# Attention scores with two heads side by side in the rows of TensorE's array

## The chip, the cores and the metric

One core of one Trainium2 chip runs the whole kernel in one launch. The metric is the time on the device in microseconds (us); the times below are those of single executions of the same kernel. One further execution was profiled; the rows come from it.

## The reference, cut to what matters

Three layers are computed one after the other for 1536 tokens: attention with a local window, a gated layer, and a mixture of 8 experts of which each token takes two. The change is in the attention:

```
B, H, S, D = q.shape                      # 2, 8, 768, 64
scores = matmul(q, k.T) / sqrt(D)
keep   = (column < n_global) | ((row - column >= 0) & (row - column < n_local))   # 8, 96
scores = where(keep, scores - slope[h] * dist, -1e9)
a      = exp(scores - max);  a /= sum(a) + 1e-9
x      = matmul(a, v)                     # then: rms norm, gate/value/out, experts
```

## The kernel before, in words

A tile `ti` is 128 tokens (12 tiles: 2 batches of 6). Because of the window, a tile looks at 256 columns of keys (`W`): 32 columns that hold the first keys of the batch, the end of the tile before, and its own 128. The first tile of each batch looks at 128. Tiles 0 to 5 (`F32T` is 6) work in fp32, where a product of the program is two matmul records in the profile; tiles 6 to 11 split each operand into a high and a low part in fp32r and add three products (`prods`), one record each.

A slot is two heads of one tile, so there are 4 slots to a tile and 48 in all, `u = 4 * ti + pr`. For a tile, `prep` turns k and q so that the head dimension lies on partitions: two heads of 64 share the 128 partitions of one block (4 blocks for 8 heads). For a slot, `scores` multiplies, VectorE adds the bias and takes the maximum (L436), ScalarE takes exp (L439); `turn` (fp32) or a DMA (`dma_start_transpose`, L448, on SP's queue) turns the result, and `values` multiplies with v. At a tile's end come rms norm (its power on POOL, L585) and `norm`, which turns x for the next layer.

How the two heads reach the array. In tile 0 (`ti < HALF`), a head's 64 partitions of q and of k are multiplied as they lie, so a matmul uses half of the array's rows; `pair` puts heads h and h + 2 in a slot, and both have the same half. In tiles 1 to 11, q is held in two copies (`qtile`), one for even and one for odd heads, in which the other head's 64 partitions are zero; the matmul then uses all 128 rows, and the zeros keep the other head out. The copies' zeros are written once by POOL (L345, L347), and `prep` fills each copy's other half by an operation of its own: high part on ScalarE or VectorE (L387, L389), low part on VectorE (L395).

PSUM has 8 banks, named by tag: `g`, `v`, `s`, `t`, `t2`, `o` and two of `d`. The first 12 slots (`START`, the call's `wide`) run before the next layer begins, in an order written out in `early` (every TensorE instruction follows the one before it, `seq`). There the scores of a slot (both heads in one bank) alternate between `g` and `s`, and q is turned in a `d` bank. From slot 12 on, the work of the attention is mixed with that of the next layer (`VISITS`, lines 698 to 745, which holds `g`, `v` and both `d`), in an order that a planner makes from its own estimate of times; scores then have the bank `s` alone, and all transposes share `t` and `t2`. Each engine works off its instructions in the order of the program. `busy` adds matmuls on zeros in the first slots. The tag `pt`, two buffers, holds the turned exp values between `turn` or the DMA and `values`, which comes up to three slots later (L540).

Of the kernel before, what the change touches and what calls it, by code (L numbers as in the profile page):

```python
# [10 lines left out]
F32 = mybir.dt.float32  # L11
F32R = mybir.dt.float32r
F16 = mybir.dt.float16
# [8 lines left out]
P = 128  # L22
# [85 lines left out]
def fused(ctx: ExitStack, tc: tile.TileContext, q, k, v, n_global, n_local, w_gate, w_val, w_out,  # L108
# [8 lines left out]

    def pair(ti, pr):

        a, b = (pr // 2, pr % 2) if ti < HALF else (pr % 2, pr // 2)  # L120
        return (4 * a + b, 4 * a + b + 2)
    DC = DM // P
# [12 lines left out]
    START = 12  # L135
    HALF = 1
    WARM = 4
# [26 lines left out]
    def build_bias():  # L164
        rel = sb.tile([P, 2 * P], F32, name="rel", tag="n2", bufs=N2)
        msk = sb.tile([P, 2 * P], F32, name="msk", tag="s", bufs=4)
        work = at.tile([P, 2, 2 * P], F32, name="work", tag="p", bufs=2)
        tmp, rel0, msk0 = work[:, 0], work[:, 1, :P], work[:, 1, P:]
        nc.gpsimd.iota(rel, pattern=[[-1, 2 * P]], base=P, channel_multiplier=1,
                       allow_small_or_imprecise_dtypes=True)  # L170
        nc.vector.tensor_scalar(msk, rel, 0.0, None, op0=ALU.is_ge)
        nc.vector.tensor_scalar(tmp, rel, float(n_local), None, op0=ALU.is_lt)
        nc.vector.tensor_mul(msk, msk, tmp)
        nc.vector.tensor_scalar(rel0, rel[:, P:], -float(n_local), None, op0=ALU.add)
        nc.vector.tensor_mul(rel0, rel0, msk[:, P:])
        nc.vector.tensor_scalar(rel0, rel0, float(n_local), None, op0=ALU.add)
        nc.vector.tensor_copy(msk0, msk[:, P:])
        if n_global > 0:
            nc.vector.memset(msk0[:, :n_global], 1.0)
            nc.vector.memset(rel[:, :n_global], float(n_local))  # L180
            nc.vector.memset(msk[:, :n_global], 1.0)
        if n_global < 32:
            nc.vector.memset(msk[:, n_global:32], 0.0)
        nc.vector.tensor_scalar(msk, msk, -BIG, BIG, op0=ALU.mult, op1=ALU.add)
        nc.vector.tensor_scalar(msk0, msk0, -BIG, BIG, op0=ALU.mult, op1=ALU.add)
        nc.vector.tensor_add(rel0, rel0, msk0)
        for h in (0, 2, 1, 3, 4, 6, 5, 7):
            nc.vector.tensor_scalar(nbias0[:, h, :], rel0, slopes[h], None, op0=ALU.mult)
        nc.vector.tensor_add(rel, rel, msk)
        return rel  # L190
# [49 lines left out]
    def busy(k):  # L240

        if k and state.get("strict"):
            pz = ps.tile([P, 512], F32, name="idle", tag="v")
            for _ in range(k):
                seq(nc.tensor.matmul(pz.rearrange("p (a b) -> p a b", a=4), blank,
                                     blank.rearrange("p (o d) -> p o d", o=1).broadcast_to([P, 4, P]), start=True, stop=True))
# [51 lines left out]

    cyc = {"s": 0, "t": 0, "o": 0, "d": 0}

    def bank(kind, wide, name):
        tags = {"s": ("g", "s"), "t": ("t", "t2"), "o": ("o", "d"), "d": ("d",)} if wide else {"s": ("s",), "t": ("t", "t2"), "o": ("o",)}
        cyc[kind] += 1
        tag = tags[kind][cyc[kind] % len(tags[kind])]
        return ps.tile([P, 512], F32, name=name, tag=tag, bufs=2 if tag == "d" else 1)

# [28 lines left out]

    def qtile(x, m, ti):

        key = x, m, ti // NB
        if key not in qz:
            one = m == "e"  # L340
            full = ti < F32T
            qz[key] = t = at.tile([P, NP, P], F32 if full else F32R, name=f"q{x}{m}{ti}", tag=f"q{x}{m[0]}", bufs=1 if one else 2)
            r = slice(D, P) if one else slice(0, D)
            if full:
                zero = nc.gpsimd.memset(t[r], 0.0)  # L345
            else:
                zero = nc.gpsimd.tensor_scalar(t[r], ident[r].rearrange("p (o d) -> p o d", o=1).broadcast_to([D, NP, P]),  # L347
                                               0.0, None, op0=ALU.mult)
            follow(zero.ins, state["pool"])
        return qz[key]  # L350

    def prep(ti, wide, hook=None):
# [9 lines left out]
        else:  # L362
            kT = [at.tile([P, NP, 2 * P], F32R, name=f"kT{ti}_{x}", tag=f"kT{x}", bufs=2) for x in range(2)]
        if ti < HALF:
            qa = at.tile([P, NP, P], F32, name=f"qT{ti}", tag="q1o", bufs=2)
            qT = {(0, h): qa[(h % 2) * D:(h % 2 + 1) * D, h // 2, :] for h in range(H)}
            qd = [(slice(0, P), qa, None)]
        else:
            qb = [[qtile(x, m, ti) for m in ("e", f"o{ti % 2}")] for x in range(1 if full else 2)]
            qT = {(x, h): qb[x][h % 2][:, h // 2, :] for x in range(len(qb)) for h in range(H)}  # L370
            qd = [(slice(m * D, (m + 1) * D), qb[0][m], qb[-1][m]) for m in range(2)]
        operands = ((kn, [(slice(0, P), kT[0][:, :, P:], kT[1][:, :, P:])], 1.0), (qn, qd, -(D ** -0.5)))
        p3s = {}
        state["cur", ti] = (W, C0, nblk, kT, qT)
        for step, (cs, src, dst, sc) in enumerate([(slice(0, NP),) + o for o in operands] if ti else
# [4 lines left out]
            if sc not in p3s:  # L380
                p3s[sc] = bank("t" if sc == 1.0 or not wide else "d", wide, f"pt{ti}").rearrange("p (a b) -> p a b", a=NP)
            p3 = p3s[sc]
            for c in range(cs.start, cs.stop):
                seq(nc.tensor.transpose(p3[:, c, :], src.rearrange("p (a t) d -> p a (t d)", a=NP)[:, c, :], ident))  # L384
            for n, (rs, dh, dl) in enumerate(dst):
                if wide and n:
                    nc.vector.tensor_scalar(dh[rs, cs], p3[rs, cs], sc, None, op0=ALU.mult)  # L387
                else:
                    nc.scalar.activation(dh[rs, cs], p3[rs, cs], AF.Copy, scale=sc)  # L389
                if full:  # L390
                    continue
                if sc == 1.0:
                    nc.vector.tensor_sub(dl, p3, dh.bitcast(F32))
                else:
                    nc.vector.scalar_tensor_tensor(dl[rs], p3[rs], sc, dh[rs].bitcast(F32), op0=ALU.mult, op1=ALU.subtract)  # L395

# [15 lines left out]
    def scores(u, wide):  # L412
# [6 lines left out]
        nb = nbias if ti % NB else nbias0  # L419
        psc = bank("s", wide, f"ps{ti}_{pr}")  # L420
        first = ti < F32T
        if first:
            pp = at.tile([P, 2, 2 * P], F32, name=f"p{ti}_{pr}", tag="p", bufs=2)
        else:
            pp = at.tile([P, 2, 2, W], F16, name=f"h{ti}_{pr}", tag="p", bufs=2)
        for t in range(2):
            h = pair(ti, pr)[t]
            sl = slice((h % 2) * D, (h % 2 + 1) * D) if ti < HALF else slice(0, P)
            o = psc[:, t * W:(t + 1) * W]
            prods = ((0, 0), (1, 0), (0, 1)) if ti >= F32T else ((0, 0),)  # L430
            for n, (a, c) in enumerate(prods):
                seq(nc.tensor.matmul(o, qT[a, h], kT[c][sl, h // 2, C0:], start=(n == 0), stop=(n == len(prods) - 1)))  # L432
        for t in range(2):
            h = pair(ti, pr)[t]
            s = sb.tile([P, 2 * P], F32, name=f"s{ti}_{h}", tag="s", bufs=4)
            state["s"] = nc.vector.tensor_tensor_reduce(s[:, :W], nb[:, h, :], psc[:, t * W:(t + 1) * W], 1.0, BIG * 10,  # L436
                                                        op0=ALU.add, op1=ALU.min, accum_out=mx[:, h:h + 1]).ins
# [6 lines left out]
        if first:  # L444
            state["p", u] = pp
            return
        both = at.tile([P, 2, 2, nblk, P], F16, name=f"ph{ti}_{pr}", tag="pt", bufs=2)
        nc.sync.dma_start_transpose(both.rearrange("p x t j q -> p (x t j) q"), pp.rearrange("p x t c -> p (x t c)"))  # L448
        state["pt", u] = both[:, 0], both[:, 1]

    def turn(u, wide):
        ti, pr = divmod(u, NP)
        nblk = state["cur", ti][2]
        pp = state.pop(("p", u))
        ptt = bank("t", wide, f"pp{ti}_{pr}")
        p4 = ptt.rearrange("p (t j q) -> p t j q", t=2, j=2)
        for t in range(2):
            for j in range(nblk):
                seq(nc.tensor.transpose(p4[:, t, j, :], pp[:, t, j * P:(j + 1) * P], ident))
        pf = at.tile([P, 2, 2, P], F32, name=f"pf{ti}_{pr}", tag="pt", bufs=2)  # L460
        if pr % 2 == 0:
# [9 lines left out]
    def values(u, wide):  # L471
# [15 lines left out]
        if pr == 0:  # L487
            state["po", ti] = bank("o", wide, f"po{ti}")
        po = state["po", ti]
        for t in range(2):  # L490
            h = pair(ti, pr)[t]
            hs = slice(h * D, (h + 1) * D)
# [52 lines left out]
    def early(n):  # L545
# [19 lines left out]
        if n < NP:  # L565
            for h in pair(0, n):
                follow(nc.vector.tensor_scalar(nbias[:, h, :], rel, slopes[h], None, op0=ALU.mult).ins, state["s"])
# [27 lines left out]
    def norm(ti, x, wide):  # L595
        pt = bank("t", wide, f"px{ti}")
        p3 = pt.rearrange("p (a b) -> p a b", a=DC)
# [564 lines left out]
    n = 0  # L1162
# [224 lines left out]
```

## Time and profile before

| | |
|---|---|
| time, median of 3 runs | 762.61 us (761.08 to 763.19) |
| the profiled execution's own time | 762.32 us |
| its span, first to last instruction | 760.5 us |
| TensorE busy (matmul) | 735.9 us, 97% of the span |
| weight loads | 666.6 us, 88% |
| VectorE, ScalarE, POOL busy | 485.8, 410.2, 318.8 us |

Attention ends about 195 us into the span; the rest is the two expert layers. A busy TensorE is counted from modelled ends of matmuls that overlap, so the distance between the starts of two records tells more than their durations.

### The profile page before, as it was taken

The numbers are of one execution on the slowest core, as the hardware profiler recorded it, in microseconds if no ns is written. First come the engines' busy times: TensorE is split into PE (matmuls) and PEld (weight loads), VectorE is DVE, ScalarE is ACT, GpSimd is POOL, SyncE is SP. The second block draws the span as 40 slices with busy tenths as digits, with TensorE's granted clock in tenths as the row PEclk, the third lists the DMA queues.
The fourth block names the chain that finished last, engine by engine and source line by source line (L and its number), as shares of the span: only waits on it lengthen the run. The fifth ranks groups of instructions, "written<-read, shape, count | busy, mean of one in ns | idle before, by whom it ended". The sixth has DMA issues, their size and how long they took to land.

```text
span 760.5 us, 13550 instructions
## 1 busy us (share of the span) xinstructions
PE 735.9 (97%) x4763; PEld 666.6 (88%) x4763; DVE 485.8 (64%) x1134; ACT 410.2 (54%) x878; POOL 318.8 (42%) x350
## 2 busy tenths in 40 slices
PE   9999989999999999999999999999999999999993
PEld 6788989889988888889999989888999999999993
DVE  5998899885497888334535568844555646665641
ACT  5777778675454443114332456536676757776630
POOL 3348853421476566001543144562234345353411
PEclk9999999999999999999999999999999999999997
DMA  8454457533243840002234511989396979898611
GB/s 199 126 166 126 119 135 152 97 85 70 89 135 111 250 137 1 1 6 106 56 57 91 188 29 49 310 240 281 88 264 186 281 175 285 206 323 169 212 41 37
DMA packets 183159, 107.98 MB, mean 142 GB/s; under 512 B 114193, under 2 KB 165393, under 8 KB 183088
## 3 DMA queue, kind: packets, MB, share of 16 engines
q1 hardware_dynamic: 174240, 84.61, 43.0%
q0 software_dynamic: 7120, 19.32, 7.8%
q10 hardware_dynamic: 1728, 3.15, 1.3%
q8 instruction: 39, 0.64, 0.4%
q14 instruction: 32, 0.26, 0.1%
HBM read 75.23 MB, written 16.49 MB: 121 GB/s over the span
## 4 chain that ended last, share of the span: by engine, by line
PE 79%; DVE 7%; DMA 5%; issue 4%; ACT 2%; POOL 1%; SPq 0%; POOLq 0%; ACTq 0%; DVEq 0%
PE pz L1041 17%; PE pz L705 14%; PE acc L732 12%; PE ac L1081 11%; PE pg L705 5%; PE pv L705 5%; PE ac L1058 5%; PE ps L432 3%; PE po L500 1%; DMA ph<-h 1%; PE lg L816 1%; DMA rv<-in_moe_w_val_dram 1%; PE pt L384 1%; PE po L496 1%; DMA y<-out_dram,ic 1%
## 5 line engine op out<-in xcount | busy, mean ns | idle before, releaser
L1041 PE MATMUL pz<-gh,sa 128*128 128x256 f32 (+7 forms) x576 | 154.0, 335 | 2.0 <-POOL sa L686 1.3
L1041 PEld LDWEIGHTS pz<-gh,sa 128*128 128x128 f32 x576 | 103.6, 188 | 7.3 <-POOL sa L686 1.8
L1041 PE MATMUL pz<-gl,sa 128*128 128x256 f32 (+7 forms) x288 | 96.4, 335 | 0.0
L732 PE MATMUL acc<-wo,dh 128*128 128x512 f32 x288 | 88.8, 399 | 0.7 <-ACT dh L718 0.5
L1081 PE MATMUL ac<-zh,sb 128*128 128x480 f32 (+4 forms) x320 | 84.7, 357 | 0.0
L1048 ACT ACTIVATE zh<-pz 128x256 fp32r<-128x256 f32 (+7 forms) x72 | 35.2, 488 | 80.5 <-PE pz L1041 80.5
L1049 DVE SCALAR_TENSOR_TENSOR zl<-pz,zh 128x256 fp32r<-128x256 f32 (+7 forms) x72 | 39.7, 552 | 58.3 <-ACT zh L1048 58.0
L705 PE MATMUL pz<-xTh,wg 128*128 128x256 f32 x352 | 73.9, 286 | 1.3 <-ACT wg L653 1.3
L705 PE MATMUL pz<-xTh,wv 128*128 128x256 f32 x352 | 73.6, 287 | 0.0
L1114 POOL DMA_INDIRECT out_dram<-y,me x30 | 34.2, 1141 | 72.6 <-DVE y L1110 68.7
L1081 PEld LDWEIGHTS ac<-zh,sb 128*128 128x128 f32 x320 | 59.6, 188 | 3.2
L705 PEld LDWEIGHTS pz<-xTh,wg 128*128 128x128 f32 x352 | 58.3, 190 | 3.8 <-ACT wg L653 1.5
L719 POOL TENSOR_TENSOR dl<-u,dh 128x256 fp32r<-128x256 f32 (+1 forms) x38 | 36.9, 972 | 56.6 <-ACT dh L718 31.9
L686 DVE TENSOR_TENSOR sb<-wab,sb 128x512 fp32r<-128x512 f32 x67 | 47.4, 707 | 19.7 <-ACT sb L682 16.8
L686 DVE TENSOR_TENSOR sa<-wab,sa 128x512 fp32r<-128x512 f32 x60 | 44.6, 745 | 23.6 <-ACT sa L682 23.1
L682 ACT ACTIVATE sa<-wab 128x512 fp32r<-128x512 f32 x72 | 44.9, 625 | 27.4 <-PE ac L1081 14.0
L732 PEld LDWEIGHTS acc<-wo,dh 128*128 128x128 f32 x288 | 51.2, 189 | 9.3 <-ACT dh L718 0.7
L705 PEld LDWEIGHTS pz<-xTh,wv 128*128 128x128 f32 x352 | 57.9, 190 | 0.3
L1041 PEld LDWEIGHTS pz<-gl,sa 128*128 128x128 f32 x288 | 54.1, 188 | 2.6 <-DVE gl L1013 0.3
L732 PE MATMUL acc<-wo,dl 128*128 128x512 f32 x144 | 53.5, 397 | 0.0
L1081 PE MATMUL ac<-zl,sb 128*128 128x480 f32 (+4 forms) x160 | 52.4, 358 | 0.0
L1058 PE MATMUL ac<-sb,zh 128*128 128x512 f32 (+1 forms) x176 | 50.6, 375 | 0.0
(255 smaller groups left out, 1841.8 us busy)
## 6 DMA issues: line engine op xcount, KB each, us to landing
wab<-in_moe_w_dram SPq DMA_DIRECT2D x128, 256.0 KB, 6.3
rg<-in_moe_w_gate_dram SPq DMA_DIRECT2D x12, 512.0 KB, 4.5
rv<-in_moe_w_val_dram SPq DMA_DIRECT2D x12, 512.0 KB, 3.6
ro<-in_moe_w_out_dram SPq DMA_DIRECT2D x12, 512.0 KB, 3.6
vn<-in_v_dram SPq DMA_DIRECT2D x12, 256.0 KB, 3.8
out_dram<-zero SPq DMA_DIRECT2D x1, 3072.0 KB, 14.0
x2d<-x ACTq DMA_DIRECT2D x12, 256.0 KB, 5.0
x2p<-hw SPq DMA_DIRECT2D x12, 256.0 KB, 4.6
```

Of the source, the lines that this page charges most:

```text
L432: seq(nc.tensor.matmul(o, qT[a, h], kT[c][sl, h // 2, C0:], start=(n == 0), stop=(n == len(prods) - 1)))
L682: cp = nc.scalar.activation(wp[:, 0], src, AF.Copy)
L686: sub = (nc.gpsimd if pool else nc.vector).tensor_sub(wp[:, 1], src, wp[:, 0].bitcast(F32))
L705: mm = nc.tensor.matmul(pz, a[:, cs], x[:, tt:tt + nt, c, :], start=(n == 0), stop=(n == 3 * DC - 1))
L719: (nc.gpsimd if ci < len(CHUNKS) - 1 else nc.vector).tensor_sub(dl, u, dh.bitcast(F32))
L732: nc.tensor.matmul(acc[t], a[:, tt], w, start=(f == CHUNKS[ci][0] and n == 0), stop=(end and n == 2))
L1041: mm = nc.tensor.matmul(pz[:, :cap], a[:, cs], x[:, c, :cap], start=(k == 0), stop=(k == 3 * DC - 1))
L1048: self.act = nc.scalar.activation(dh[:, :cap], pz[:, :cap], AF.Relu).ins
L1049: nc.vector.scalar_tensor_tensor(dl[:, :cap], pz[:, :cap], 0.0, dh[:, :cap].bitcast(F32), op0=ALU.max, op1=ALU.subtract)
L1058: mm = nc.tensor.matmul(o, a[:, s * P:s * P + m], w[:, cuts(s)[x]], start=(f == 0 and k == 0), stop=(f == FB2 - 1 and k == 2)).ins
L1081: nc.tensor.matmul(acc[c][:, :cap], w[:, c * P:(c + 1) * P], a[:, :cap], start=(f == 0 and k == 0), stop=(f == FB2 - 1 and k == 2))
L1114: st = nc.gpsimd.indirect_dma_start(out=out, out_offset=bass.IndirectOffsetOnAxis(ap=self.me[:m, s, 0:1], axis=0), in_=y[:m], in_offset=No ...
```

## The change

All tiles use the half of the array in which a head's partitions lie. The zero-padded copies of q (`qtile`), `pair` and `HALF` are gone; a slot holds heads 2 * pr and 2 * pr + 1, which lie in the two different halves, and their products are issued in turn, one for each head. The two heads write to two different banks: pairs (`g`, `s`) and (`v`, one `d`) alternate in the first 12 slots, and (`s`, `t2`) is the only pair afterwards, so that transposes have `t` alone from there on. The other `d` bank of the first slots (`spare`) serves `busy` and every second output of `values`; q is turned in `t` or `t2`. From slot 12 on, the first product of a slot waits for the VectorE operation that read the last scores and for the low part of q, and the other products follow in order. `prep` has one operation for the high part of q and one for the low part, over all 128 partitions. The tag `pt` has three buffers.

```diff
-    def qtile(x, m, ti):
...
+    def score_banks(u, wide):
+        if ("ps", wide) not in state:
+            tags = (("g", "s"), ("v", "d")) if wide else (("s", "t2"),)
+            state["ps", wide] = [[ps.tile([P, 512], F32, name=f"ps{u}{x}", tag=x, bufs=2 if x == "d" else 1) for x in xs] for xs in tags]
+        banks = state["ps", wide]
+        return banks[u % len(banks)]
...
+    def bank(kind, name):
+        tags = ("t", "t2") if ("ps", False) not in state else ("t",)
+        cyc[kind] += 1
+        if kind == "o":
+            return spare() if state.get("strict") and cyc[kind] % 2 == 0 else ps.tile([P, 512], F32, name=name, tag="o")
+        return ps.tile([P, 512], F32, name=name, tag=tags[cyc[kind] % len(tags)])
...
-        if ti < HALF:
-            qa = at.tile([P, NP, P], F32, name=f"qT{ti}", tag="q1o", bufs=2)
...
-            qb = [[qtile(x, m, ti) for m in ("e", f"o{ti % 2}")] for x in range(1 if full else 2)]
+        qa = [at.tile([P, NP, P], F32 if full else F32R, name=f"qT{ti}_{x}", tag=f"q{x}", bufs=2) for x in range(1 if full else 2)]
+        qT = {(x, h): qa[x][(h % 2) * D:(h % 2 + 1) * D, h // 2, :] for x in range(len(qa)) for h in range(H)}
...
-            for n, (rs, dh, dl) in enumerate(dst):
-                if wide and n:
-                    nc.vector.tensor_scalar(dh[rs, cs], p3[rs, cs], sc, None, op0=ALU.mult)
...
+            dh, dl = dst
+            nc.scalar.activation(dh[:, cs], p3[:, cs], AF.Copy, scale=sc)
+            if not full:
+                state["prepped", ti] = nc.vector.scalar_tensor_tensor(dl[:, cs], p3[:, cs], sc, dh[:, cs].bitcast(F32), op0=ALU.mult,
+                                                                      op1=ALU.subtract).ins
...
+        out_s = [b[:, :W] for b in score_banks(u, wide)]
...
+        for n, (a, c) in enumerate(prods):
+            for t in range(2):
+                mm = seq(nc.tensor.matmul(out_s[t], qT[a, 2 * pr + t], kT[c][t * D:(t + 1) * D, pr, C0:], start=(n == 0),
+                                          stop=(n == len(prods) - 1))).ins
+                if not state.get("strict"):
+                    if n or t:
+                        follow(mm, state["mm"])
+                    else:
+                        for x in (state["s"], state.get(("prepped", ti))):
+                            if x is not None:
+                                hold(mm, x)
+                    state["mm"] = mm
-            for n, (a, c) in enumerate(prods):
-                seq(nc.tensor.matmul(o, qT[a, h], kT[c][sl, h // 2, C0:], start=(n == 0), stop=(n == len(prods) - 1)))
...
-        both = at.tile([P, 2, 2, nblk, P], F16, name=f"ph{ti}_{pr}", tag="pt", bufs=2)
+        both = at.tile([P, 2, 2, nblk, P], F16, name=f"ph{ti}_{pr}", tag="pt", bufs=3)
...
-        pf = at.tile([P, 2, 2, P], F32, name=f"pf{ti}_{pr}", tag="pt", bufs=2)
+        pf = at.tile([P, 2, 2, P], F32, name=f"pf{ti}_{pr}", tag="pt", bufs=3)
```

## Rows read from the trace of the kernel before

**Rows 1.** The page: busy us per engine, and the last chain's shares by engine.
```profile
PE 735.9 (97%) x4763; PEld 666.6 (88%) x4763; DVE 485.8 (64%) x1134; ACT 410.2 (54%) x878; POOL 318.8 (42%) x350
...
PE 79%; DVE 7%; DMA 5%; issue 4%; ACT 2%; POOL 1%; SPq 0%; POOLq 0%; ACTq 0%; DVEq 0%
```

**Rows 2.** Busy us by stretch: PE, PEld, DVE, ACT, POOL, granted clock, DMA share, GB/s.
```profile
36.00:95.00 59.00, 56.30 (x421) 52.26 (x421) 50.38 (x135) 44.25 (x120) 41.82 (x43) 1.00 0.51 141
...
104.00:190.00 86.00, 83.25 (x906) 77.87 (x906) 68.17 (x203) 59.16 (x180) 28.21 (x39) 1.00 0.49 102
190.00:760.00 570.00, 555.21 (x3183) 504.31 (x3181) 331.68 (x668) 277.54 (x492) 232.55 (x222) 0.99 0.52 147
```

**Rows 3.** Waits of PE, first 190 us: us in total, times, longest.
```profile
PE po L500 <- DMA ph<-h: 1.5, 2, 0.9
PE ps L432 <- DVE mx L436: 1.3, 2, 1.1
PE pz L705 <- ACT wg L653: 1.3, 1, 1.3
...
PE px L599 <- DVE x L586: 1.1, 1, 1.1
PE pp L459 <- DVE pf L464: 1.0, 1, 1.0
PE pp L459 <- DVE xTl L605: 0.7, 1, 0.7
PE po L496 <- ACT pf L462: 0.5, 1, 0.5
```

**Rows 4.** The chain that ended last, first 190 us: start us, us, what.
```profile
39.39 0.70 DVE q0o L387
...
60.74 0.86 PE ps L432 x4
...
107.97 2.29 DMA ph<-h
...
127.70 0.71 PE ps L432 x6
...
166.44 4.22 DMA ph<-h
```

**Rows 5.** Timeline at the score matmuls of tile 0's last slot and of tile 1.
```profile
14.33 0.28 PE L496 MATMUL po<-vn,pf 128*128 128x64 f32 x1
14.54 0.18 PEld L432 LDWEIGHTS ps<-kT,qT 64*128 64x128 f32 x1
...
14.75 0.49 PE L432 MATMUL ps<-kT,qT 64*128 64x128 f32 x3
...
14.97 0.27 PE L432 MATMUL ps<-kT,qT 64*128 64x128 f32 x1
15.17 0.10 PEld L245 LDWEIGHTS <-zero 128*128 128x128 bf16 x1
15.18 0.39 PE L245 MATMUL idle<-zero 128*128 128x512 bf16 x1
...
18.08 0.28 PE L496 MATMUL po<-vn,pf 128*128 128x64 f32 x1
...
18.19 0.43 PE L432 MATMUL ps<-kT,q0e 128*128 128x256 f32 x1
```

**Rows 6.** Lines that fill or clear q: duration ns min/median/max, first and last start.
```profile
L387 DVE TENSOR_SCALAR q0o<-pt x3: 694/695/695, 14.9 to 39.4; 64x512 f32<-64x512 f32 x3
...
L389 ACT ACTIVATE q0o<-pt x8: 592/593/596, 50.9 to 159.1; 64x512 fp32r<-64x512 f32 x6, 64x512 f32<-64x512 f32 x2
...
L395 DVE SCALAR_TENSOR_TENSOR q1o<-pt,q0o x6: 694/694/696, 84.9 to 160.9; 64x512 fp32r<-64x512 f32 x6
...
L347 POOL TENSOR_SCALAR q0o<-ident x2: 1934/1936/1937, 70.4 to 87.4; 64x512 fp32r<-64x512 f32 x2
```

**Rows 7.** Waits of SP's own queue, whole span: us in total, times, longest.
```profile
SPq L448 <- PE po L500: 6.5, 6, 2.1
```

More of the change, by code (lines that the diff above doesn't have):

```diff
@@ L116, in fused @@
     NP = H // 2
-    def pair(ti, pr):
-        a, b = (pr // 2, pr % 2) if ti < HALF else (pr % 2, pr // 2)
-        return (4 * a + b, 4 * a + b + 2)
     DC = DM // P
@@ L186, in build_bias @@
         nc.vector.tensor_add(rel0, rel0, msk0)
-        for h in (0, 2, 1, 3, 4, 6, 5, 7):
+        for h in range(H):
             nc.vector.tensor_scalar(nbias0[:, h, :], rel0, slopes[h], None, op0=ALU.mult)
@@ L242, in busy @@
         if k and state.get("strict"):
-            pz = ps.tile([P, 512], F32, name="idle", tag="v")
+            pz = spare()
             for _ in range(k):
@@ L297, in halves, with spare @@
         return w[:, :, 0], w[:, :, 1]
-    cyc = {"s": 0, "t": 0, "o": 0, "d": 0}
-    def bank(kind, wide, name):
-        tags = {"s": ("g", "s"), "t": ("t", "t2"), "o": ("o", "d"), "d": ("d",)} if wide else {"s": ("s",), "t": ("t", "t2"), "o": ("o",)}
+    cyc = {"t": 0, "o": 0}
+    def bank(kind, name):
+        tags = ("t", "t2") if ("ps", False) not in state else ("t",)
         cyc[kind] += 1
-        tag = tags[kind][cyc[kind] % len(tags[kind])]
-        return ps.tile([P, 512], F32, name=name, tag=tag, bufs=2 if tag == "d" else 1)
+        if kind == "o":
+            return spare() if state.get("strict") and cyc[kind] % 2 == 0 else ps.tile([P, 512], F32, name=name, tag="o")
+        return ps.tile([P, 512], F32, name=name, tag=tags[cyc[kind] % len(tags)])
+    def spare():
+        if "spare" not in state:
+            state["spare"] = ps.tile([P, 512], F32, name="spare", tag="d", bufs=2)
+        return state["spare"]
+    def score_banks(u, wide):
[4 more added lines that the diff above has]
+        return banks[u % len(banks)]
     def load_qk(ti):
@@ L334, in vsplit @@
         return vn, rn
-    def qtile(x, m, ti):
[L338 to L350, printed above, removed]
     def prep(ti, wide, hook=None):
@@ L363, in prep @@
             kT = [at.tile([P, NP, 2 * P], F32R, name=f"kT{ti}_{x}", tag=f"kT{x}", bufs=2) for x in range(2)]
-        if ti < HALF:
-            qa = at.tile([P, NP, P], F32, name=f"qT{ti}", tag="q1o", bufs=2)
-            qT = {(0, h): qa[(h % 2) * D:(h % 2 + 1) * D, h // 2, :] for h in range(H)}
-            qd = [(slice(0, P), qa, None)]
-        else:
-            qb = [[qtile(x, m, ti) for m in ("e", f"o{ti % 2}")] for x in range(1 if full else 2)]
-            qT = {(x, h): qb[x][h % 2][:, h // 2, :] for x in range(len(qb)) for h in range(H)}
-            qd = [(slice(m * D, (m + 1) * D), qb[0][m], qb[-1][m]) for m in range(2)]
-        operands = ((kn, [(slice(0, P), kT[0][:, :, P:], kT[1][:, :, P:])], 1.0), (qn, qd, -(D ** -0.5)))
+        qa = [at.tile([P, NP, P], F32 if full else F32R, name=f"qT{ti}_{x}", tag=f"q{x}", bufs=2) for x in range(1 if full else 2)]
+        qT = {(x, h): qa[x][(h % 2) * D:(h % 2 + 1) * D, h // 2, :] for x in range(len(qa)) for h in range(H)}
+        operands = ((kn, (kT[0][:, :, P:], kT[1][:, :, P:]), 1.0), (qn, (qa[0], qa[-1]), -(D ** -0.5)))
         p3s = {}
@@ L380, in prep @@
             if sc not in p3s:
-                p3s[sc] = bank("t" if sc == 1.0 or not wide else "d", wide, f"pt{ti}").rearrange("p (a b) -> p a b", a=NP)
+                p3s[sc] = bank("t", f"pt{ti}").rearrange("p (a b) -> p a b", a=NP)
             p3 = p3s[sc]
@@ L384, in prep @@
                 seq(nc.tensor.transpose(p3[:, c, :], src.rearrange("p (a t) d -> p a (t d)", a=NP)[:, c, :], ident))
-            for n, (rs, dh, dl) in enumerate(dst):
-                if wide and n:
-                    nc.vector.tensor_scalar(dh[rs, cs], p3[rs, cs], sc, None, op0=ALU.mult)
[L388 to L395, printed above, removed]
+            dh, dl = dst
[3 more added lines that the diff above has]
+                                                                      op1=ALU.subtract).ins
         def same(dst, src):
@@ L419, in scores @@
         nb = nbias if ti % NB else nbias0
-        psc = bank("s", wide, f"ps{ti}_{pr}")
+        out_s = [b[:, :W] for b in score_banks(u, wide)]
         first = ti < F32T
@@ L425, in scores @@
             pp = at.tile([P, 2, 2, W], F16, name=f"h{ti}_{pr}", tag="p", bufs=2)
-        for t in range(2):
[L427 to L430, printed above, removed]
-            for n, (a, c) in enumerate(prods):
-                seq(nc.tensor.matmul(o, qT[a, h], kT[c][sl, h // 2, C0:], start=(n == 0), stop=(n == len(prods) - 1)))
-        for t in range(2):
-            h = pair(ti, pr)[t]
+        prods = ((0, 0), (1, 0), (0, 1)) if ti >= F32T else ((0, 0),)
+        for n, (a, c) in enumerate(prods):
[10 more added lines that the diff above has]
+                    state["mm"] = mm
+        for t in range(2):
+            h = 2 * pr + t
             s = sb.tile([P, 2 * P], F32, name=f"s{ti}_{h}", tag="s", bufs=4)
-            state["s"] = nc.vector.tensor_tensor_reduce(s[:, :W], nb[:, h, :], psc[:, t * W:(t + 1) * W], 1.0, BIG * 10,
+            state["s"] = nc.vector.tensor_tensor_reduce(s[:, :W], nb[:, h, :], out_s[t], 1.0, BIG * 10,
                                                         op0=ALU.add, op1=ALU.min, accum_out=mx[:, h:h + 1]).ins
@@ L454, in turn @@
         pp = state.pop(("p", u))
-        ptt = bank("t", wide, f"pp{ti}_{pr}")
+        ptt = bank("t", f"pp{ti}_{pr}")
         p4 = ptt.rearrange("p (t j q) -> p t j q", t=2, j=2)
@@ L487, in values @@
         if pr == 0:
-            state["po", ti] = bank("o", wide, f"po{ti}")
+            state["po", ti] = bank("o", f"po{ti}")
         po = state["po", ti]
         for t in range(2):
-            h = pair(ti, pr)[t]
+            h = 2 * pr + t
             hs = slice(h * D, (h + 1) * D)
@@ L565, in early @@
         if n < NP:
-            for h in pair(0, n):
+            for h in (2 * n, 2 * n + 1):
                 follow(nc.vector.tensor_scalar(nbias[:, h, :], rel, slopes[h], None, op0=ALU.mult).ins, state["s"])
@@ L595, in norm @@
     def norm(ti, x, wide):
-        pt = bank("t", wide, f"px{ti}")
+        pt = bank("t", f"px{ti}")
         p3 = pt.rearrange("p (a b) -> p a b", a=DC)
```

1 line of the change is left out of this document (removed).

## The prediction

> **What bounds the kernel now.** I read the page first. TensorE is busy 97% of the span, no other engine over 64%, and the last chain is 79% TensorE [rows 1]. Then the stretches: the change touches only the first 190 us, and there too TensorE is nearly full, 56.3 of 59 us and 83.3 of 86 us at full granted clock [rows 2]. After 190 us the same matmuls follow whatever happened before, so the end moves by as much as the attention does. Third, TensorE's own waits in those 190 us: the seven listed come to 1.5 + 1.3 + 1.3 + 1.1 + 1.0 + 0.7 + 0.5 = 7.4 us, each for a VectorE or ScalarE operation or for turned exp values [rows 3]. That is the whole stock from which relief of other engines can pay. What the change does to TensorE's own time counts nearly in full.
>
> **TensorE: what a slot of scores costs now.** The chain shows an fp32 slot (two heads, four records of 256 columns) at 0.86 us, 0.216 per record, and an fp32r slot (six records) at 0.71 us, 0.118 per record [rows 4]. There are 20 slots of fp32 outside tile 0 and 24 of fp32r, four of these with 128 columns; I count them alike.
>
> **What the half-array form costs.** Only tile 0 uses it now, with both heads in one half, so it shows the price of entering and leaving, and nothing of two halves at work together. In tile 0's last slot the matmul before starts at 14.33, the weight load at 14.54, the second record at 14.75; records follow each other every 0.11 here (three from 14.75, the last at 14.97), so the first ran from 14.64, 0.31 after the one before. In tile 1, in the full form, the same step takes 18.08 to 18.19, 0.11. Entering costs 0.20. On leaving, the last record starts at 14.97 and the next matmul at 15.18: 0.21 in place of 0.11, so 0.10, and this with a short bf16 weight load (0.10) behind it [rows 5]. An fp32 load would stand open for up to 0.11 more. Together 0.30 to 0.41 us a slot; I take 0.35. No wait of that size is listed there; the array empties before the other form's weights go in.
>
> The Trainium skill (TensorEngine Tiling (Array Packing), Key Properties) says the same: to change the tiling mode, not merely the tile, drains TensorE. It speaks against this change, which switches 88 times more than before, and gives no price. If a switch were free, the sum below would be about 0.35 x 44 = 15 us lower than it is; the trace agrees with the rule.
>
> **Do the halves work side by side?** No row shows it. The bounds: not at all, then each slot keeps its record times and pays 0.30 to 0.41 more; or wholly. I take the overlap, since what serialises tile 0's records, one half and one bank for both heads, is taken away, and the array already loads weights beneath a running matmul (a load of 0.18 with records 0.11 apart [rows 5]).
>
> - fp32r: products alternate between the halves, three steps in place of six: 3 x 0.118 + 0.30 to 0.41 = 0.65 to 0.76, against 0.71. I take no change; ends over 24 slots -1.4 and, without overlap, 24 x 0.41 = +9.8.
> - fp32: a product is two records, and both of one head come before the other head's, so only the inner two overlap: 3 x 0.216 + 0.35 = 1.00 against 0.86, +0.14 x 20 = +2.8. Ends: all four overlap in pairs, 2 x 0.216 + 0.30 = 0.73, -2.6; none, 0.41 x 20 = +8.2.
> - tile 0 pays its switches already and has one record of 0.11 less in each of four slots: -0.4 (0 to -0.9).
>
> TensorE: 0 + 2.8 - 0.4 = **+2.4 us** (-4.9 to +18).
>
> The Trainium skill (TensorE: Matmul & The Clock Gate, Part 3, packing small matmuls) states that matmuls in different row groups start about 4 ns apart and run together. By it, an estimate, three pairs take some 12 ns more than three single steps, 0.3 us over 24 slots. No row of this kernel shows it either way.
>
> **Relief of the other engines.** VectorE loses nine operations of 0.69 (three L387, six L395), 6.2 us; ScalarE eight of 0.59, 4.7 us [rows 6]. POOL loses its clearing of q, six operations of up to 1.94. POOL's I cost at nothing: it is busy 28 to 42 us of 59 and 86 [rows 2], and its share of the chain is 1% [rows 1]; were it late, the keys' copies in front of a tile's first slot would be late next. The third `pt` buffer lets SP issue the turning DMA without waiting for `values`; SP waited for that 6.5 us in all, six times [rows 7]. Two of the chain's stretches are such DMAs (107.97 and 166.44, [rows 4]).
>
> What this gives TensorE is bounded by its 7.4 us of waits [rows 3]. Item by item: of the 1.5 for turned values 0.7 (one of the two, the other was VectorE's lateness); of the 1.3 for VectorE's maximum 1.1, since two operations of 0.69 go from VectorE's queue ahead of it; of the 1.3 for a converted weight 0.7, since L387 at 39.39 is in the chain that leads to it [rows 4]; the 1.1 for x, whose v was loaded late behind SP's queue; 0.7 of the 1.0 for L464; 0.3 of the 0.7; 0.4 of the 0.5. Sum **-5.0 us** (0 to -7.4).
>
> **Banks.** From slot 12 on, transposes have one bank in place of two: four transposes, then the copies out (0.59 and 0.69), before the next may begin. There are 38 such uses in about 150 us. Waits for this already exist with two banks, 1.0 and 0.7 for L464 and L605 [rows 3]; I take half as much again, **+0.9 us** (0 to +3.4, twice as much again). Behind such a wait all of TensorE's queue stands, so the layer's matmuls (L705) are late next, and TensorE's extra time hides part of it. The scores' own banks cost nothing: one bank for two heads before, one pair now, released by the same VectorE operation. The new wait for the low part of q costs nothing: the second product needed it 0.12 us later anyway. The smaller load on VectorE covers it; without this cover a tile's first slot, six times, would wait up to 0.69.
>
> **Sum.** The profiled execution took 762.3 us, its span 760.5 and 1.8 around it, and stands 0.3 below the median of the runs, 762.6. 2.4 - 5.0 + 0.9 = -1.7: 760.6 for that execution, **760.9 us** on the median. 0.3% is 2.3 us, about what a measurement of this kernel can tell from no change; the likeliest case ends just inside it.
>
> **Rivals.**
>
> 1. *The weight loads of the two halves queue up.* Then matmuls overlap but loads come one by one, 0.11 apart as in tile 0's rows [rows 5]. An fp32r slot takes 6 x 0.11 + 0.30 to 0.41 = 0.96 to 1.07, +0.30, over 24 slots +7.2; fp32 stays at +2.8, where two loads fit beneath each record of 0.216. 7.2 - 1.7 = +5.5: 768. It decides against the change from 0.17 more per fp32r slot, (2.3 + 1.7) / 24. For it: the records, each with a load of its own, are never closer than that in tile 0. Against it: all these loads go to the same rows. The Trainium skill (TensorE: Matmul & The Clock Gate, LDWEIGHTS) says that a load's time goes by its columns, not its rows; the load of 64 rows took 0.18 [rows 5], which does not contradict it.
> 2. *No overlap at all.* 44 x 0.35 = 15.4, less 0 for tile 0, -5.0, +0.9: +11, 774. The change would then not do what it says.
> 3. *More overlap, and the waits gone.* All four fp32 records in pairs (-2.6), fp32r 0.03 below now (-0.7), tile 0 -0.9, waits -5.0, banks +0.9: -8.3, 754.
> 4. *The banks bind, or the planner's new order loses what was gained.* +3.4 in place of +0.9, half of the relief: +2.4 - 2.5 + 3.4 = +3.3, 766. For it: TensorE has little slack. Against: two of its seven waits are of this kind.
>
> **How the numbers follow.** Likeliest case 0.42, own range 757 to 764 (relief 0 to -7.4 against banks 0 to +3.4, not both at their ends): 0.21 faster, 0.18 same, 0.03 slower. Rival 1 0.20 (0.02 of it same), rival 2 0.09, rival 3 0.17 (faster), rival 4 0.12 (0.05 same, 0.07 slower). Faster 0.38, same 0.25, slower 0.37. The range 754.5 to 771 leaves out rival 2 (0.09) and about half of rival 3 (0.08).
>
> **What would show it.** Right: score records of 64 rows in all tiles; in fp32r the two heads' records start almost together and the six span about 0.35; the step into the first is 0.3, the step after the last 0.2; one operation each for q on ScalarE and VectorE; TensorE's waits for L436, L586 and turned values shorter. Wrong: six starts 0.11 apart (rivals 1, 2); steps at the switch well under 0.2; fp32 records of one head overlapping the other's fully (rival 3); new waits of TensorE in front of L384, L459 or L599 (rival 4). The prediction fails by most if the switch costs another amount than in tile 0's one slot at this clock, for it is paid 44 times.

## The result, and the profile after

The changed kernel takes 770.67 us (769.01 to 774.24, 4 runs) where the kernel before, beside it, takes 762.9: a ratio of 1.0106 [1.0056, 1.0155]: about 1% slower, and clear of its interval. A second measurement, among the experiments, gave 1.0124 [1.0094, 1.0154]. The forecast was 760.9, a little faster. That 770.67 still lies inside the range of 754.5 to 771 is no support for the sum: the range was drawn that wide for rivals, 1 and 4 among them.

The page of the profiled execution after (769.26 us, span 767.6): engine shares, and the last chain, which answer to [rows 1].

```profile
PE 735.7 (96%) x4763; PEld 651.5 (85%) x4763; DVE 480.9 (63%) x1125; ACT 405.3 (53%) x870; POOL 306.5 (40%) x341
...
PE 76%; DVE 7%; DMA 6%; issue 4%; ACT 3%; POOL 2%; SPq 1%; POOLq 0%; ACTq 0%; DVEq 0%
```

The other engines were relieved, about as forecast: 4.9 us on VectorE (forecast 6.2), 4.9 on ScalarE (4.7), 12.3 on POOL. TensorE has the same busy time in a span that is 7 us longer. The loss can be placed. The 745th matmul record of the first expert layer starts at 228.28 us before and at 236.18 after, 7.9 later; the difference stays at 7.9 through the rest of that layer and is 7.1 at the end of the span. Busy us up to that record (columns as in [rows 2]), before:

```profile
0.00:228.28 228.28, 218.97 (x1847) 197.25 (x1848) 181.49 (x508) 151.66 (x425) 110.29 (x153) 1.00 0.50 125
```

and after:

```profile
0.00:236.18 236.18, 218.68 (x1847) 181.97 (x1848) 176.72 (x499) 146.63 (x417) 96.32 (x144) 0.99 0.51 121
```

TensorE ran the same 1847 records in 0.3 us less and stood idle 17.5 us in place of 9.3. The 7.9 us are idle time of TensorE (+8.2); its own work, all in all, did not become dearer. Its waits in the first 237 us after, the answer to [rows 3]:

```profile
PE po L487 <- DMA ph<-h: 2.3, 3, 0.8
PE px L586 <- DVE qT L375: 1.6, 1, 1.6
PE pz L692 <- ACT wv L640: 1.5, 2, 0.9
PE acc L719 <- ACT dh L705: 1.4, 2, 1.2
...
PE pt L371 <- DVE pf L451: 1.2, 1, 1.2
PE pz L692 <- ACT xTh L591: 0.9, 1, 0.9
...
PE pt L371 <- DVE ss L570: 0.7, 1, 0.7
PE pp L446 <- ACT qT L373: 0.7, 1, 0.7
PE pz L692 <- DVE u L702: 0.7, 2, 0.5
...
PE acc L719 <- POOL dl L706: 0.6, 1, 0.6
```

Read them in three kinds. L371, L446 and L586 are transposes that wait for a bank, 1.6 + 1.2 + 0.7 + 0.7 (the 1.2 of L371 and the 0.7 behind `ss` in the first slots, at 21 and 33 us). L487 waits for turned exp values, as before. The layer's own matmuls (L692, L719) wait for converted weights, for the last tile's x and for their own results; those from 200 us on (1.2 for `dh`, 0.9 for `xTh`, 0.7 for `u`, 0.6 for `dl`) have no counterpart before, where no wait of TensorE is listed from 190 to 230 us. The last record of attention's last transposes (L586; before L599) starts at 210.6 us, before at 202.0.

**The halves work side by side.** The timeline of TensorE at an fp32 slot after, the answer to [rows 4] and [rows 5]:

```profile
61.83 0.49 PE L446 MATMUL pp<-ident,p 128*128 128x128 f32 x3
62.25 0.48 PE L410 MATMUL ps12s<-kT,qT 64*128 64x256 f32 x1
62.26 0.48 PE L410 MATMUL ps12t<-kT,qT 64*128 64x256 f32 x1
62.57 0.38 PE L410 MATMUL ps12s<-kT,qT 64*128 64x256 f32 x1
62.58 0.38 PE L410 MATMUL ps12t<-kT,qT 64*128 64x256 f32 x1
62.88 0.39 PE L692 MATMUL pz<-xTh,wv 128*128 128x256 f32 x1
```

its weight loads:

```profile
62.25 0.18 PEld L410 LDWEIGHTS ps12s<-kT,qT 64*128 64x128 f32 x1 [0.17 <-DVE mx L423]
62.26 0.18 PEld L410 LDWEIGHTS ps12t<-kT,qT 64*128 64x128 f32 x1
62.36 0.19 PEld L410 LDWEIGHTS ps12s<-kT,qT 64*128 64x128 f32 x1
62.37 0.19 PEld L410 LDWEIGHTS ps12t<-kT,qT 64*128 64x128 f32 x1
```

and an fp32r slot:

```profile
131.65 0.40 PE L692 MATMUL pz<-xTh,wg 128*128 128x256 f32 x2
131.97 0.38 PE L410 MATMUL ps12s<-kT,qT 64*128 64x256 f32 x1
131.98 0.38 PE L410 MATMUL ps12t<-kT,qT 64*128 64x256 f32 x1
132.20 0.28 PE L410 MATMUL ps12s<-kT,qT 64*128 64x256 f32 x1
132.20 0.28 PE L410 MATMUL ps12t<-kT,qT 64*128 64x256 f32 x1
132.32 0.27 PE L410 MATMUL ps12s<-kT,qT 64*128 64x256 f32 x1
132.32 0.27 PE L410 MATMUL ps12t<-kT,qT 64*128 64x256 f32 x1
132.52 0.72 PE L719 MATMUL acc<-wo,dh 128*128 128x512 f32 x2
```

`ps12s` and `ps12t` are the two banks of a pair, one for each head. Both heads' records, and their weight loads, start at most 0.01 us apart, the fp32 ones too: an fp32 slot is two steps (62.25, 62.57, then 62.88), an fp32r slot three. The fp32 slot takes 0.63 us and 0.10 more at its entry: 0.73 in place of 0.86 in [rows 4]. The fp32r slot takes 132.52 - 131.97 = 0.55, and enters 0.20 after the last record of the group at 131.65 (131.77) where 0.12 would be usual: 0.63 in place of 0.71. Over 20 and 24 slots that is 20 x 0.13 + 24 x 0.08 = 4.5 us less, and 4.9 with the 0.4 forecast for tile 0.

**The clock.** Busy us and granted clock around the longest new wait:

```profile
112.00:114.00 2.00, 1.10 (x16) 0.86 (x15) 1.32 (x3) 1.28 (x3) 0.00 (x0) 1.00 0.75 74
114.00:116.00 2.00, 1.33 (x20) 1.11 (x20) 1.20 (x6) 1.62 (x8) 0.55 (x1) 1.00 0.58 131
116.00:118.00 2.00, 0.36 (x4) 0.30 (x3) 1.88 (x10) 1.72 (x8) 1.55 (x4) 0.50 0.57 132
118.00:120.00 2.00, 2.00 (x11) 1.44 (x10) 0.54 (x4) 0.60 (x1) 0.24 (x1) 0.50 0.87 196
120.00:122.00 2.00, 2.00 (x17) 1.87 (x17) 1.82 (x6) 1.68 (x6) 1.85 (x2) 0.50 0.29 66
122.00:124.00 2.00, 2.00 (x15) 1.89 (x13) 1.32 (x3) 0.73 (x2) 0.00 (x0) 0.79 0.29 67
```

TensorE's records around the wait:

```profile
115.81 0.27 PE L410 MATMUL ps12t<-kT,qT 64*128 64x128 f32 x1
117.73 0.66 PE L586 MATMUL px<-ident,x 128*128 128x128 f32 x2 [1.64 <-DVE qT L375]
```

The norm's transposes (L586) wait 1.64 us for the bank that VectorE frees of q (L375). The clock is at half (1.2 GHz) from 116.0 to 122.8, so it fell when this wait began and not behind it. Ahead of the fall, from 112 us on, TensorE was busy 1.10 and 1.33 us of two each and had waited twice for 0.78 us (from 112.6 and from 113.9 on, the second time for turned exp values). Of the 6.8 us at half clock TensorE worked in the last 5.1, from 117.73 on; at most half of them, 2.6 us, is the price. This is part of the 218.68 us of busy time, and one reason why 4.9 us of cheaper scores show as 0.3. In the repeated measurement's profile the same wait and a half clock of the same length stand again, the wait from 113.2 and the half clock from 114.2 us on. Before, this stretch is at full clock [rows 2].

The profiled executions are no accident. The mean granted clock over all executions of the change is 0.986 in both measurements (4 and 5 executions), that of the kernel before beside the second one 0.992 (20 executions). An estimate from these, time x (1 - clock) in each execution, gives at most 10.7 us lost to the clock in the change and 6.4 before: up to 4.3 of the 9.4 us by which the means of the second measurement differ.

### The profile page after: what moved, and what is told of

Read it like the earlier page. It is cut to its first block, busy times and chain, and to the rows that moved or that the text cites. A ratio compares the mean times of both kernels' runs of the same rounds, so it can differ in the third digit from the quotient of the medians.

```text
span 767.6 us, 13537 instructions
## 1 busy us (share of the span) xinstructions
PE 735.7 (96%) x4763; PEld 651.5 (85%) x4763; DVE 480.9 (63%) x1125; ACT 405.3 (53%) x870; POOL 306.5 (40%) x341
## 4 chain that ended last, share of the span: by engine, by line
PE 76%; DVE 7%; DMA 6%; issue 4%; ACT 3%; POOL 2%; SPq 1%; POOLq 0%; ACTq 0%; DVEq 0%
PE pz L1028 16%; PE pz L692 14%; PE acc L719 11%; PE ac L1068 10%; PE pg L692 5%; PE pv L692 5%; PE ac L1045 5%; PE ps12s L410 2%; DMA wab<-in_moe_w_dram 2%; PE po L487 2%; DMA ph<-h 1%; PE lg L803 1%; DMA ro<-in_moe_w_out_dram 1%; PE pt L371 1%; DVE s L423 1%
## 5 line engine op out<-in xcount | busy, mean ns | idle before, releaser
L719 PE MATMUL acc<-wo,dh 128*128 128x512 f32 x288 | 88.3, 399 | 1.9 <-ACT dh L705 1.9
L692 PE MATMUL pz<-xTh,wg 128*128 128x256 f32 x352 | 74.6, 289 | 2.0 <-ACT xTh L591 0.9
L692 PE MATMUL pz<-xTh,wv 128*128 128x256 f32 x352 | 74.0, 287 | 2.3 <-ACT wv L640 1.5
L692 PEld LDWEIGHTS pz<-xTh,wg 128*128 128x128 f32 x352 | 58.6, 192 | 7.2 <-DVE u L702 1.5
L692 PEld LDWEIGHTS pz<-xTh,wv 128*128 128x128 f32 x352 | 57.9, 190 | 3.5 <-ACT wv L640 1.9
L719 PEld LDWEIGHTS acc<-wo,dh 128*128 128x128 f32 x288 | 51.1, 189 | 11.4 <-ACT dh L705 2.8
L719 PE MATMUL acc<-wo,dl 128*128 128x512 f32 x144 | 53.0, 401 | 0.6 <-POOL dl L706 0.6
L692 PE MATMUL pz<-xTl,wg 128*128 128x256 f32 x176 | 51.0, 290 | 0.2 <-DVE xTl L592 0.2
```

What stands on the lines that cost most here:

```text
L692: mm = nc.tensor.matmul(pz, a[:, cs], x[:, tt:tt + nt, c, :], start=(n == 0), stop=(n == 3 * DC - 1))
L719: nc.tensor.matmul(acc[t], a[:, tt], w, start=(f == CHUNKS[ci][0] and n == 0), stop=(end and n == 2))
```

## The experiments

Theory A throughout: after slot 12 the single transposes bank is what costs. B, C and D name the rival of a run and are told in its expectation. Ratios are to the kernel before on the same chip. TensorE's idle time is 200 us less its busy time in the window 36:236 of the profiled execution. The position is the number of the layer's matmul records (lines L705 and L732 before) that stand in TensorE's order ahead of the first score of slots 24 and 47. The change, e13 and e2 have three `pt` buffers, all others two. The idle time of e5 is left out, as the mean clock of its profiled execution was 0.97; the profiled executions of e9 and e14 have half clock from 18 to 39 us (769.2 us against a median of 763.9, 776.7 against 772.6), and their idle times compare less well.

| kernel | ratio | idle, us | before slot 24 | before slot 47 |
|---|---|---|---|---|
| before | 1 | 6.7 | 128 | 474 |
| the change | 1.0106 | 13.1 | 194 | 538 |
| the change, again (e13) | 1.0124 [1.0094, 1.0154] | 13.0 | 194 | 538 |
| the change without `hold` (e2) | 1.0113 [1.0060, 1.0166] | 5.8 | 186 | 497 |
| the change, two `pt` buffers (e5) | 1.0079 [1.0046, 1.0113] | | 194 | 509 |
| half rows in tiles 0 to 2 (e3) | 0.9938 [0.9911, 0.9965] | 4.9 | 128 | 478 |
| in tiles 0 to 2 and 6 to 11 (e10) | 0.9952 [0.9918, 0.9987] | 5.1 | 156 | 521 |
| in tiles 0 to 5 (e9) | 1.0025 [0.9996, 1.0054] | 8.0 | 157 | 524 |
| from tile 3 on (e8) | 1.0125 [1.0081, 1.0169] | 11.2 | 194 | 509 |
| before, one bank (e1) | 1.0050 [1.0020, 1.0081] | 8.5 | 162 | 516 |
| e3, one bank in tiles 3 to 5 (e12) | 1.0082 [1.0043, 1.0121] | 10.1 | 138 | 524 |
| before, handed out later (e4) | 1.0103 [1.0061, 1.0146] | 10.4 | 126 | 535 |
| e10, handed out later (e14) | 1.0063 [1.0036, 1.0089] | 11.3 | 156 | 541 |
| e10, one pair in the first slots (e15) | 1.0045 [1.0022, 1.0068] | 10.7 | 156 | 532 |

### One bank, and nothing else

```diff
-  ... else {"s": ("s",), "t": ("t", "t2"), "o": ("o",)}
+  ... else {"s": ("s",), "t": ("t",), "o": ("o",)}
```

> The kernel before with one thing taken from the change: from slot 12 on, transposes have one bank (t) in place of two. Scores stay in the full form. Theory A (the lost bank binds: TensorE waits for copies out of t, and the planner, which knows of the bank, issues attention later): slower by 5 to 11 us, ratio 1.007 to 1.014, the same late order of the slots and waits of TensorE in front of L384, L459 and L599. Rival B (the half-array form itself loses the time, by its switches): within 2 us of before, ratio 0.998 to 1.003.

1.0050, between A's 1.007 and B's 1.003: the bank costs, and less than the whole loss. The slots stand later, but not as late as in the change.

### No waits put in by hand

The lines with `hold` go from `scores`.

> The changed kernel without the two added waits of a slot's first product (for the last scores' VectorE operation and the low part of q); the products still follow each other. Theory A: within 2.5 us of the changed kernel, ratio to before 1.007 to 1.014. Rival C (the added waits hold up TensorE's queue, with everything behind them): at least 4 us of the loss comes back, ratio below 1.006.

1.0113 [1.0060, 1.0166]: no time is recovered, but rival C is not settled by it. Without `hold` the first record of a slot is often issued alone, ahead of the others; the 49 runs of score records in TensorE's order become 70, each with a switch. Busy us up to the 745th record of the first expert layer:

```profile
0.00:236.84 236.84, 226.05 (x1848) 185.93 (x1848) 176.49 (x499) 145.50 (x417) 97.23 (x144) 0.99 0.48 120
```

TensorE is idle 10.8 us there in place of 17.5, and busy 7.4 us more; 21 more switches at some 0.28 us, the price worked out below, would be 5.9 of them, by an estimate. So waits went and switches came. That kernels without `hold` lose time too is shown by e1 and e12.

### Half rows in the first twelve slots alone

The kernel before with `HALF = 3`, natural pairs, and the change's two score pairs, `spare` and q in `t`/`t2` for tiles 0 to 2; from tile 3 on as before.

> Halves only in the 12 slots of tiles 0 to 2, with their two pairs of banks and one operation each for q; from tile 3 on all as before, with two banks for transposes. Theory A: the half form itself pays and the loss lies after slot 12, so faster than before by 1 to 3 us, ratio 0.996 to 0.999. Rival B: 12 slots with a switch loss of 0.3 each, 2 to 4 us slower, ratio 1.002 to 1.005.

0.9938: faster than both kernels, and by more than A gave (0.996). The loss lies behind slot 12.

### The third buffer taken back

`bufs=3` of `pt` back to 2 in the changed kernel.

> The changed kernel with two buffers for turned weights, as before. If the third buffer pays what the prediction gave it (0.7 us and part of 1.1 us), 1 to 2 us slower than the changed kernel, ratio to before 1.010 to 1.016; if VectorE's lateness decides, as fast as the changed kernel within 1 us.

1.0079 [1.0046, 1.0113], beside 1.0106 and 1.0124 with three: the third buffer gives nothing that shows. It changes the order all the same: the last slot stands behind 509 of the layer's records with two buffers, behind 538 with three.

### The change from slot 12 on

Tiles 1 and 2 in full rows with the banks of before, tile 0 as before; `pt` with two buffers.

> The kernel before in slots 0 to 11 (tile 0 in its one half, tiles 1 and 2 full rows, one bank for two heads, two for transposes) and the change from slot 12 on (half rows, the pair s and t2, one transposes bank, scores behind the last maximum). The remainder of the change when the first-twelve run (0.994) is taken out. If the parts add up: 1.0106 / 0.994 = 1.017 (1.012 to 1.022). Rival, the early slots only bring work forward into the same later wait, so that their gain is not lost in the whole change but never adds: 1.011 (1.007 to 1.012).

1.0125, at the lower end of the sum's range and just past the upper end of the rival's. Beside the whole change (1.0106, 1.0124), what the first slots gain when they are alone (0.6%) is not to be seen. But the kernel to compare with is e5, which has two `pt` buffers too and the same positions: there it is 1.0125 / 1.0079 = 0.5%, as the parts would have it. The intervals leave both open.

### Half rows in the fp32 tiles, or in the fp32r tiles

e3 with the change's `scores` and `qT` in tiles 3 to 5, or 6 to 11, and there the pair (`s`, `t2`) and one transposes bank:

```diff
+        elif ti in HV:
+            state["one"] = True
+            out_s = [ps.tile([P, 512], F32, name=f"ps{u}{x}", tag=x)[:, :W] for x in ("s", "t2")]
         else:
+            state["one"] = False
```

> The first-twelve kernel with half rows and the pair s and t2 in the fp32 tiles 3 to 5 also (slots 12 to 23, one transposes bank there); full rows, one score bank and two transposes banks from tile 6 on. Theory A, the loss goes by the time with one transposes bank, most of it where attention is densest (slots 12 to 23, fp32, q and exp both turned on TensorE): 0.994 + 0.010 = 1.004 (1.000 to 1.008). Theory B, the loss comes in the fp32r tiles, where the planner puts the slots far behind: 0.994 less twelve slots of 0.13 us, 0.992 (0.989 to 0.996).

> The first-twelve kernel with half rows and the pair s and t2 in the fp32r tiles 6 to 11 also (slots 24 to 47, one transposes bank there); full rows and two transposes banks in slots 12 to 23. Here slot 25 stands behind 227 of the layer's matmuls where the first-twelve kernel has it behind 138: the scores wait for the bank t2. Theory A (loss where attention is densest, slots 12 to 23): 0.994 + 0.004 = 0.998 (0.994 to 1.002). Theory B (loss in the fp32r tiles and by the late order): 0.994 + 0.015 = 1.009 (1.003 to 1.014).

1.0025 and 0.9952: of the two stretches taken alone, the loss comes in slots 12 to 23, as A has it. There a tile's exp values are turned on TensorE, so that four slots use the bank seven times (k, q, four times exp, x); in the fp32r tiles a DMA turns exp, and there are three uses.

### One bank in the fp32 tiles, in full rows

e3 with one line changed; `scores` sets `state["tile"]`.

```diff
-        tags = {"s": ("s",), "t": ("t", "t2"), "o": ("o",)}
+        tags = {"s": ("s",), "t": ("t",) if 3 <= state.get("tile", 0) < 6 else ("t", "t2"), "o": ("o",)}
```

> The first-twelve kernel with one thing more: a single transposes bank in the fp32 tiles 3 to 5; full rows and one score bank there, no hold. The planner's order of the slots from 19 on is that of the run with half rows in those tiles, within ten of the layer's matmuls. Theory A, the bank (with the order that it brings) is what costs there: 1.0025 plus twelve slots of 0.13 us that half rows had saved, 1.0045 (1.001 to 1.008). Theory D, the bank is nearly free and the switches and the wait of the scores for the last maximum cost: 0.994 (0.990 to 0.998).

1.0082, at the upper end of A: 1.0082 / 0.9938 = 1.4% for one bank in twelve slots. The half rows in the same slots (e9) take 1.0025 / 1.0082 = 0.6% of it back; the 0.13 us a slot of the forecast would be 0.2%, and the intervals reach that far. Waits of TensorE in this kernel, from 36 us on:

```profile
PE ps L452 <- DVE mx L456: 2.3, 2, 1.8
...
PE ps L452 <- ACT wcv L660: 1.2, 1, 1.2
PE pp L479 <- ACT pf L482: 1.2, 2, 1.0
PE pp L479 <- DVE xTl L625: 0.7, 1, 0.7
```

Only the last two are the bank itself (L479, transposes of exp), 1.9 us of a price of some 11; the scores wait more. The bank puts slots behind in TensorE's order, and most of its price is paid elsewhere. It is no fixed price: in e1 the same bank, taken from all slots from 12 on, cost 0.5%.

### The place alone

`LAG` is how many slots of attention are handed to the planner ahead of the layer's passes: 0 in place of 8 in the kernel before (e4), 4 in place of 8 in e10 (e14).

> The kernel before with one constant changed, so that attention's slots are handed to the planner eight slots later against the layer's passes: full rows, two transposes banks, no switch. Slot 32 stands behind 288 of the layer's matmuls (before 228, the change 302), the last behind 535 (474 and 538). Theory C, that attention ending late is in itself what costs (the next layer waits for the last tile): 1.006 (1.004 to 1.012), the idle time of TensorE near its end 3 us more. Theory A, it is the bank and not the place: 1.000 (0.997 to 1.003).

> The kernel with half rows in tiles 0 to 2 and 6 to 11 (0.995), its slots from 27 on handed to the planner four later: slots 29 to 34 stand 10 to 22 of the layer's matmuls further back, the last behind 541 (before this 521, the change 538). Theory C, attention ending late costs by itself: 1.002 (0.999 to 1.007). Theory A, with two banks where exp is turned on TensorE a late end is free: 0.995 (0.992 to 0.998).

1.0103 and 1.0063 (1.0063 / 0.9952 = 1.1%): with two transposes banks where exp is turned, an order in which attention ends later costs about as much as the whole change. A late place in the middle does not: e10 has slot 32 behind 315 of the layer's records (the change 302, before 228) and is fast. Where the late order costs is not the same in the two. In e4 it is mostly scores behind late maxima:

```profile
PE ps L432 <- DVE mx L436: 4.6, 3, 1.8
PE po L500 <- DMA ph<-h: 2.4, 2, 1.5
```

In e14 a good part is the end of attention, as in the changed kernel; its waits from 200 to 230 us:

```profile
PE acc L778 <- ACT dh L764: 1.2, 1, 1.2
PE pz L751 <- DVE u L761: 1.2, 2, 0.6
PE pz L751 <- ACT xTh L650: 0.9, 1, 0.9
```

The last tile's x (`xTh`) is late, and so few of the layer's matmuls are left to put in front that each waits for its own chain (`u`, `dh`). In e10 no such wait is listed from 195 us on. But this execution of e14 is the one with half clock early on, and 2.3 us of its waits, for late maxima at 77 and 80 us, stand ahead of slot 27, the first that was moved; they are not the edit's.

### One pair of banks in the first slots

e10 with (`g`, `s`) alone in slots 0 to 11, and q turned in `d`.

> The same kernel (tiles 0 to 2 and 6 to 11 in half rows, 0.995) with one pair of score banks in place of two in the first twelve slots, and q turned in a bank of its own there, as before the change. If the second pair carries the early gain: each of eleven slots waits for the last slot's two maxima, some 0.6 us, 1.004 (1.000 to 1.008). If the early gain is the half rows' and q's wait for t and t2 (1.6 us in the first-twelve run) is the larger loss: 0.994 (0.991 to 0.997).

1.0045: without the second pair the gain is gone. But the waits expected in the first slots are not there; TensorE waits later, 4.1 us of it for turned exp values:

```profile
PE po L547 <- DMA ph<-h: 4.1, 4, 1.7
PE pz L752 <- ACT wg L700: 2.2, 2, 1.4
PE po L543 <- DVE vn L516: 1.6, 1, 1.6
```

How the first slots bring this about stays open, and so does whether the pair or the new order costs.

### The change once more

> The change as it stands, once more beside its parts. If the costs of the two stretches with one bank add: 0.994 x (1.0025 / 0.994) x (0.995 / 0.994) = 1.004 (1.000 to 1.008). If the second stretch costs only where the first has already put the slots behind: 1.011 (1.008 to 1.015).

1.0124: the parts, as run, do not add up to the change. The second stretch with one bank, 0.1% by itself (e10 against e3), would have to cost about 1.0% behind the first (the change's 1.0124 against e9's 1.0025). But the parts have two `pt` buffers and the change has three. With two, the parts give 1.0025 x 0.9952 / 0.9938 = 1.0039, and the whole (e5) 1.0079, a difference that lies within the intervals. Whether the rest comes with the second stretch or with the third buffer is open. The waits of this repetition are those shown above, at nearly the same times.

## Why the prediction was wrong

- **The price of a switch: right, at its lower end or just below.** Over its two steps of 0.216 the fp32 slot takes 0.73 - 0.43 = 0.30 more, over its three of 0.12 the fp32r slot 0.63 - 0.36 = 0.27; 0.30 to 0.41 was forecast and 0.35 taken. The first record in tile 0's last slot started at 14.54 with its weights, not at 14.64 as the forecast had it; the second came 0.21 later, so that the price of entering was the same 0.20, half of it within the slot.
- **Overlap: better than taken.** The fp32r slot is at 0.63 against a range of 0.65 to 0.76; the fp32 slot at 0.73, the lowest of the ends named, where 1.00 was taken: the array issues both heads' first record, then both heads' second. TensorE's term of +2.4 came out near -4.9. Rivals 1 and 2 are out. The Trainium skill (TensorE: Matmul & The Clock Gate, Part 3, packing small matmuls) has matmuls of different row groups start about 4 ns apart; the rows above, up to 0.01 us apart, agree with it. The weight loads of the two halves start as close.
- **Relief of the other engines, -5.0: the first step that failed.** VectorE, ScalarE and POOL did get the time back, and SP's wait for the buffer of turned values [rows 7] is gone, but TensorE waits 2.3 us for turned values where it waited 1.5 [rows 3]. The list of 7.4 us was that of the old order, and the order did not stay. The third buffer shows it: with two, and otherwise the change from slot 12 on (e8), the waits for turned values are longer,

```profile
PE po L531 <- DMA ph<-h: 5.7, 3, 2.5
```

  but from 200 us on TensorE waits 0.9 us there, against 3.6 in the change, where the last slot stands later.
- **Banks, +0.9 (0 to +3.4): the step that decided.** It counted waits in front of the bank, and as such its bounds hold: the transposes' waits for a bank after slot 12 are 1.6 + 0.7 us and 0.3 more, where the 0.7 for L605 stood with two banks [rows 3]. (The 1.0 for L464, which the forecast counted with it, stood at 31 us, in the first slots.) Left out was that a planner that knows of one bank puts the slots elsewhere: slot 24 behind 194 of the layer's records in place of 128. The price then shows under other lines, as in e12. Relief and banks together were forecast at -4.1 us and came as +8.2 us of idle time.
- **"After 190 us the same matmuls follow": wrong in a part.** Attention now ends so late that the layer's next matmuls wait for it, 3.4 us in the lines above between 200 and 230 us.
- **The clock was not in the sum.** Up to 2.6 us in the profiled execution, and up to 4.3 over the executions of e13.
- **Rival 4 had the mechanism**, at 0.12 and with +3.3 us. The argument against it, that only two of seven waits were of this kind, read a list that the old order had made. The Trainium skill (TensorEngine Tiling (Array Packing), Gotcha 1: PSUM Pressure) says that row tiles write to different banks. The pair of banks for two heads follows from it; no run here put both heads in one bank.

What adds up and what does not: from the same record, -4.9 for scores, up to +2.6 for the clock and +8.2 of idle time make up to +5.9 of 7.9; the rest is not assigned. That the loss lies behind slot 12 and that one bank there costs is shown (e3, e1, e12). That the planner's order is the link between the two is borne out by e12, e4 and e14, but not isolated: no run has one bank in the old order, or the change's order with two. A rival stands beside it, untested: that any change of the planner's order can move this kernel by about 1%, whatever set it off. e4, which takes no bank, and e15 speak for it. Why the planner chose just this order was not tried. A kernel with half rows and two transposes banks in the fp32 tiles was not tried either, for want of a bank.

The best versions run are e3 and e10, 0.9938 and 0.9952: half rows with the two pairs in the first twelve slots, with or without the fp32r tiles, and full rows with two transposes banks where exp is turned on TensorE.

## What to carry to other kernels

Half-array pairs pay when the slot itself is counted, but they take a second bank; ask which other use loses it, and count that bank's uses stage by stage, not over the kernel. Where a planner sets the order, a resource that is taken away can be paid for in the new order more than in waits in front of it: compare the positions in the instruction order before reading waits. A list of waits prices the present order only. Positions are no price either: they do not rank the kernels of the table.

## What the runs showed of the hardware

- The two halves run fp32 records and fp32 weight loads in step, at most 0.01 us apart; a switch of form and back costs 0.27 to 0.30 us at full clock.
- Half clock came amid waits that a page of 768 us hardly shows. In the change it lasted 6.8 us, and it began when TensorE had waited no longer than 0.78 us at a time; the wait of 1.64 us came with it. In the trace from tile 3 on (e8) the first two stretches (36 to 95 us with waits of up to 1.2, 95 to 170 with waits of up to 2.5 for turned exp values) have mean clocks of 0.94 and 0.93:

```profile
36.00:95.00 59.00, 55.68 (x382) 46.84 (x380) 49.41 (x123) 37.64 (x99) 31.11 (x34) 0.94 0.50 142
95.00:170.00 75.00, 69.09 (x675) 60.30 (x673) 49.35 (x156) 46.72 (x145) 25.31 (x40) 0.93 0.52 98
```

  Not each wait of that size goes with it: before, the scores wait 1.1 us at 102 and TensorE is busy 0.93 us of two, at full clock throughout:

```profile
102.00:104.00 2.00, 0.93 (x6) 0.77 (x6) 2.00 (x9) 1.25 (x6) 1.92 (x5) 1.00 1.09 333
```
